# A scatter's integer places made by GpSimd instead of ScalarE, and the padding rows' scatters spread out

## The chip, the cores and the metric

The kernel runs on one core of one Trainium2 chip. The metric is the time of one execution on the device, in microseconds. A core has a matrix engine (PE, TensorE), three engines for elementwise work (DVE = VectorE, ACT = ScalarE, POOL = GpSimd) and a queue engine (SP = SyncE) that here issues most of the transfers between DRAM and on-chip memory. Each engine takes its own instructions in the order of the program; where one needs another's result it waits for a semaphore.

## What is computed

Two blocks follow each other. The first is a Fourier mixing of a batch of 8 sequences of 2496 positions with 256 features: a discrete Fourier transform along the features and one along the sequence, of which the real part is kept. The second is a mixture of experts over the resulting 19968 rows: each row goes to the one expert of 8 whose gate logit is largest, through two matrices with a ReLU between them, and is scaled by the gate's softmax weight.

```python
X = np.fft.fft(np.fft.fft(x, axis=1), axis=2).real      # x: (8, 2496, 256)
x = X.reshape(19968, 256)
logits = x @ w_gate                                     # (19968, 8)
e = argmax(logits, axis=1)
g = softmax(logits)[row, e]
out[row] = g * (maximum(x[row] @ w1[e], 0) @ w2[e])     # w1: (8, 256, 1024), w2: (8, 1024, 256)
```

## The kernel before

**Batches and rounds.** The 8 batches pass through the mixing one after the other (`first`, `regroup`, `second`), and the experts' work on batch b - 1 and older is woven with the mixing of batch b. `second` makes the mixed rows of a batch in two halves; each half has 10 tiles of 128 rows (`rows`, 258 wide: 256 values, the row's number, its gate weight). `route` (L416) finds each row's expert and, at L450 to L453, its place in the DRAM buffer `Xs`, where the rows lie sorted by expert.

**The scatters.** A tile's 128 rows go to their places by one indirect DMA from POOL, `put_row` (L235, its instruction has line L236): POOL reads 128 integers from a column of the tile `pi` and makes a transfer of them. `route` does not send at once; it appends the float place `pf`, the column of `pi` and the rows to the deque `waiting`, and `send` (L462) takes one entry off when the schedule says so. For the first batch DVE writes the integers in L453. For the other seven, ACT converts the float column to the integer column just before the scatter (L467). Seven batches of 20 tiles make 140 such conversions; the first batch has 20 scatters without one.

**When scatters are due.** The main loop (L941 to L971) steps through the experts' work and calls `send` after steps of the mixing; from batch 4 on (`LATE`, L184) a `room` count spaces them. For the batches before, an expert block that needs rows of a batch that is not yet complete makes the loop send everything that waits at once (L954 to L958). So scatters come in bursts, above all in the first three rounds.

**Reading the rows back.** `fetch_rows` (L524) has SP load a block of 512, 256 or 128 sorted rows. The first fetch of a batch waits until all its scatters have landed; later ones wait for a free buffer (`xb`, three of them). `turn` (L574) transposes the block on DVE (L580).

**Padding.** Blocks of the last round may run past an expert's rows. After the main loop, `pads` (L846) sends 8 scatters of padding rows, one for each expert, each yielding to the loop at L973: one scatter after each step of the experts' remaining work, so all eight within the first eight steps. Only the last round's blocks, fetched after it, need them.

**The last stage.** The blocks of the last round with 512 rows (`quartered`) take 21 steps each: 14 of the first layer (`seven`) and 7 of the second (`lower`). Each ends with four output scatters `out_dram<-y,ro` from POOL. POOL also makes, one block ahead, the combinations of the second layer's weights (`below`, `right`, L568 to L571) in these blocks.

**POOL's queue.** Every scatter, of rows, of padding and of output, is in one order on POOL. Each waits for the eighth scatter before it, as eight semaphores go round.

Of the kernel before, what the change touches and what calls it, by code (L numbers as in the profile page):

```python
# [12 lines left out]
F32 = mybir.dt.float32  # L13
# [202 lines left out]
def kernel(ctx: ExitStack, tc, x, w_gate, w1, w2, out):  # L216
    nc = tc.nc
    vec, act, pool = nc.vector, nc.scalar, nc.gpsimd
# [16 lines left out]
    def put_row(dst, idx, rows, last, group):  # L235
        return unordered(pool.indirect_dma_start(  # L236
            out=dst, out_offset=bass.IndirectOffsetOnAxis(ap=idx, axis=0),
            in_=rows, in_offset=None, bounds_check=last, oob_is_err=False), group)


    def sent(ins, b):
        tc.declare_no_dep(ins, group="taken", reason="no block before this batch's round has these rows")
        tc.add_to_no_dep_group(f"xs{b}", ins)
# [10 lines left out]
    sp = ctx.enter_context(tc.tile_pool(name="sp", bufs=2))  # L254
# [14 lines left out]
    con, k = {}, 0  # L269
# [192 lines left out]
    def send():  # L462

        if waiting:
            b, place, idx, rows = waiting.popleft()
            if b:
                act.copy(idx, place)  # L467
            sent(put_row(Xs, idx, rows, E * CAP - 1, "xs"), b)


# [375 lines left out]
    def pads(b):  # L846

        ti = cp.tile([128, E], I32, name="ti")
        vec.tensor_scalar(ti[:], base[:], con["lane"][:], None, op0=ALU.add)
        for e in range(E):  # L850
            sent(put_row(Xs, ti[:, e:e + 1], pad[:], ROWS - 1, "xs"), b)
            yield
# [82 lines left out]
    for k, _ in enumerate(second(0)):  # L935
        if k % 2 == 0:
            next(early, None)
        send()
    work = experts(todo)
    steps = {b: mixed(b) for b in range(1, B)}  # L940
    for b in range(1, B):  # L941

        done, due, room = 0, 0.0, 0.0
# [7 lines left out]
        while done < total:  # L951
            w, full = next(work)
            done += w
            if full and not w:  # L954

                while waiting:
                    send()
                whole.update(p[0] for p in tabs if p != "cnt")  # L958
            if not full:
                due += ticks * w / ((SHARE if b >= LATE else EARLY) * open_) if w else 1  # L960
            while due >= 1:
                next(side, None)
                due -= 1
                if b < LATE or not w:
                    send()
            room = min(room + (w if full else 0.75 * w), 2)
            if b >= LATE and room >= ROOM:
                send()
                room -= ROOM
        for _ in side:  # L970
            send()  # L971
    rest = pads(B - 1)
    for _ in work:  # L973
        next(rest, None)


_INS = ["x", "moe_w_gate", "moe_w1", "moe_w2"]
# [46 lines left out]
```

## Time and profile before

| | |
|---|---|
| median of 3 runs | 1304.29 us (1298.82 to 1309.32) |
| profiled execution | 1306.36 us, span of its instructions 1304.6 us |
| PE busy | 1227.3 us, 94% of the span |
| DVE, ACT, POOL busy | 700.7, 436.0, 361.8 us |
| scatters of rows, of padding, of output | 160, 8, 163 |
| mean granted clock of PE | 0.970 |

The profile is one execution. Its page lists each engine's busy time, a chain of waits followed back from the end, and groups of like instructions with their mean duration and the idle time of their engine before them. The timeline lists instructions with start and duration; in square brackets stands how long the engine was idle before, and what ended that. "issue" there means that the profile shows nothing that the engine waited for, "remote" that a semaphore came whose sender the profile could not match.

### The profile page before, as it was taken

Reading aid. Unit: us, or ns where it says so; the run is one execution under the profiler, and the core shown is the slowest. Engines: PE = TensorE matmul, PEld = TensorE weight load, DVE = VectorE, ACT = ScalarE, POOL = GpSimd, SP = SyncE. Lnnn points to the kernel's source line nnn. Section 1 sums busy time; section 2 is a strip of 40 time slices with the busy share of each in tenths; the row PEclk is TensorE's granted clock in tenths of the full one; section 3 lists DMA queues with packets and bytes.
Section 4 is the critical chain, followed back from the end, with each engine's and each line's share of the span. In section 5 each row is a group of like instructions: output and inputs, shape, how many; then the busy total and the mean of one; then the engine's idle time right before and its main releaser. Section 6 shows DMA issues by size and latency. Waiting matters only on the chain.

```text
span 1304.6 us, 21062 instructions
## 1 busy us (share of the span) xinstructions
PE 1227.3 (94%) x6905; PEld 1080.0 (83%) x6905; DVE 700.7 (54%) x1772; ACT 436.0 (33%) x1096; POOL 361.8 (28%) x355
## 2 busy tenths in 40 slices
PE   5668898999999999999999999999999999999996
PEld 3557797876788888888888888888889999999995
DVE  4455433433456555566546455675468774444662
ACT  1423222332334343434334343432233332222232
POOL 0245215125014311351114411351354221111112
PEclk8869898999999999999999999999999999999998
DMA  8859697657446445483335535453444238787786
GB/s 244 264 182 326 211 339 262 180 188 237 136 133 216 160 146 158 145 264 108 112 115 182 159 104 161 126 164 105 120 131 163 90 106 295 275 277 270 282 285 236
DMA packets 163210, 249.71 MB, mean 191 GB/s; under 512 B 118601, under 2 KB 130227, under 8 KB 143516
## 3 DMA queue, kind: packets, MB, share of 16 engines
q1 hardware_dynamic: 146327, 203.28, 49.0%
q0 software_dynamic: 15888, 42.14, 9.0%
q10 hardware_dynamic: 885, 2.94, 0.7%
q8 instruction: 56, 0.92, 0.3%
q14 instruction: 54, 0.44, 0.1%
HBM read 194.91 MB, written 54.83 MB: 191 GB/s over the span
## 4 chain that ended last, share of the span: by engine, by line
PE 86%; DVE 4%; DMA 4%; another core or an unknown queue 2%; issue 2%; ACT 1%; SPq 1%; POOL 0%; POOLq 0%; DVEq 0%; ACTq 0%
PE py L221 32%; PE ph L221 10%; PE c L221 10%; PE a L221 9%; PE p L221 6%; PE d L221 6%; PE b L221 5%; PE e L221 4%; PE s L221 3%; DMA w_sb<-in_moe_w_dram 2%; DMA xq<-in_x_dram 1%; DMA Td<-t 1%; SPq L532 1%; PE rk L221 0%
## 5 line engine op out<-in xcount | busy, mean ns | idle before, releaser
L221 PE MATMUL py<-w_sb,hT 128*128 128x256 f32 x2016 | 457.8, 381 | 8.3 <-DVE hT L794 8.3
L221 PEld LDWEIGHTS py<-w_sb,hT 128*128 128x128 f32 x2016 | 379.8, 191 | 59.1 <-DVE hT L794 8.7
L236 POOL DMA_INDIRECT out_dram<-y,ro x163 | 162.8, 999 | 735.8 <-ACT y L835 494.3
L236 POOL DMA_INDIRECT Xs<-rows,pi x160 | 163.5, 1022 | 199.0 <-ACT pi L467 81.6
L221 PE MATMUL ph<-xT,w_sb 128*128 128x128 f32 (+2 forms) x992 | 173.5, 330 | 9.0 <-DVE hT L794 5.3
L221 PEld LDWEIGHTS ph<-xT,w_sb 128*128 128x128 f32 x992 | 137.0, 194 | 34.3 <-issue 18.6
L835 ACT ACTIVATE y<-py,xb 128x256 f32<-128x256 f32 x129 | 61.1, 474 | 244.4 <-PE py L221 206.2
L221 PE MATMUL a<-xT,w_sb 128*128 128x256 f32 (+1 forms) x512 | 118.2, 358 | 2.1 <-ACT hT L629 1.3
L794 DVE TENSOR_SCALAR hT<-ph 128x512 f32<-128x512 f32 x43 | 29.7, 691 | 144.3 <-issue 73.6
L619 DVE TENSOR_TENSOR u<-p,b 128x512 f32<-128x512 f32 x57 | 39.2, 687 | 125.1 <-PE b L221 90.3
L221 PEld LDWEIGHTS a<-xT,w_sb 128*128 128x128 f32 x512 | 89.0, 190 | 14.7 <-ACT hT L629 2.5
L408 DVE COPY lg<-p 128x16 f32<-128x16 f32 x80 | 13.9, 174 | 142.4 <-ACT zs L405 131.8
L629 ACT ACTIVATE hT<-a 128x512 f32<-128x512 f32 x57 | 34.0, 597 | 157.7 <-PE a L221 116.7
L583 ACT ACTIVATE xT<-xT 128x256 f32<-128x256 f32 (+1 forms) x94 | 36.4, 387 | 135.3 <-DVE xT L580 88.6
L221 PE MATMUL s<-xq,w 104*112 104x256 f32 (+2 forms) x208 | 60.4, 413 | 13.1 <-DVE xq L297 12.6
L221 PEld LDWEIGHTS p<-table,t 120*128 120x128 f32 x352 | 55.3, 206 | 17.1 <-issue 6.3
L221 PE MATMUL c<-xT,ws 128*128 128x256 f32 (+1 forms) x256 | 60.5, 364 | 6.9 <-DVE hT L625 6.7
L221 PE MATMUL p<-table,t 120*128 120x120 f32 (+1 forms) x352 | 58.2, 292 | 8.3 <-ACT zz L379 3.4
L221 PE MATMUL p<-table,zz 128*128 128x145 f32 (+1 forms) x320 | 57.6, 305 | 7.8 <-issue 4.8
L580 DVE STREAM_TRANSPOSE xT<-xb 128x512 f32<-128x512 f32 (+1 forms) x94 | 58.1, 625 | 4.7 <-DMA xb<-Xs 4.7
L796 ACT ACTIVATE hT<-ph 128x512 f32<-128x512 f32 x55 | 32.8, 597 | 80.2 <-PE ph L221 59.1
L221 PE MATMUL b<-xs,ws 128*128 128x256 f32 (+1 forms) x256 | 58.7, 356 | 0.0
(145 smaller groups left out, 1739.8 us busy)
## 6 DMA issues: line engine op xcount, KB each, us to landing
w_sb<-in_moe_w_dram SPq DMA_DIRECT2D x132, 1024.0 KB
xq<-in_x_dram SPq DMA_DIRECT2D x24, 896.0 KB
xb<-Xs SPq DMA_DIRECT2D x112, 128.0 KB
Td<-t SPq DMA_DIRECT2D x18, 448.0 KB
t<-Td SPq DMA_DIRECT2D x8, 768.0 KB
t<-Td SPq DMA_DIRECT2D x8, 640.0 KB
xb<-Xs SPq DMA_DIRECT2D x52, 64.0 KB
xb<-Xs SPq DMA_DIRECT2D x100, 32.0 KB
```

The lines of the kernel that those rows point to most:

```text
L221: nc.tensor.matmul(o, lhsT=lhsT, rhs=rhs, start=start, stop=stop, **kw)
L236: return unordered(pool.indirect_dma_start(out=dst, out_offset=bass.IndirectOffsetOnAxis(ap=idx, axis=0), in_=rows, in_offset=None, bounds ...
L408: vec.tensor_copy(lg[:, k:k + 2], p3[:, NY:NY + 2 * E].rearrange("p (m e) -> p m e", m=2))
L532: taken(nc.sync.dma_start(out=flat[32 * q:32 * q + 32, 0:2 * size].rearrange("p (j e) -> p j e", e=64), in_=Xs[ds(row, size), 64 * q:64 * ...
L580: vec.transpose(free(xT[:], 256 * h, [32, n // 32], [BIG, 2], [1, 32]), free(xb, 512 * h, [64, n // 32], [1, 2], [2, 32]))
L583: act.activation(odd, odd, ACTF.Copy, scale=-1.0)
L619: vec.tensor_tensor(u2[:], p1[:], b[:], op=add)
L629: act.activation(h11, a[:], ACTF.Relu)
L794: vec.tensor_scalar(o, ph[:], 0.0, None, op0=ALU.max)
L796: act.activation(o, ph[:], ACTF.Relu)
L835: act.activation(y[:], py[:], ACTF.Copy, scale=meta[:, i, 1:2])
```

## The change

`send` gets a step more: ACT copies the float place into a small tile `due`, of which eight exist in turn, and POOL converts it into the integer column, directly before the scatter. The padding scatters are taken at every fourth step of the remaining work instead of at every one.

```diff
         if waiting:
             b, place, idx, rows = waiting.popleft()
             if b:
-                act.copy(idx, place)
+                due = sp.tile([128, 1], F32, tag="due", name="due", bufs=8)
+                act.copy(due[:], place)
+                pool.tensor_copy(idx, due[:])
             sent(put_row(Xs, idx, rows, E * CAP - 1, "xs"), b)
...
     rest = pads(B - 1)
-    for _ in work:
-        next(rest, None)
+    for k, _ in enumerate(work):
+        if k % 4 == 0:
+            next(rest, None)
```

In the built program ACT's copy now also waits for POOL's conversion of eight sends before, POOL's conversion waits for ACT's copy, and the scatter waits for POOL's own conversion. On PE, DVE and SP the order of the instructions is the same as before. On POOL four padding scatters stay in front of the second set of L568 to L571, a fifth comes behind it, and three come behind the four output scatters of the next block, in front of the third set.

## The prediction

> **What bounds the kernel.** I read the page first: engines and the chain of waits.
>
> ```profile
> span 1304.6 us, 21062 instructions
> PE 1227.3 (94%) x6905; PEld 1080.0 (83%) x6905; DVE 700.7 (54%) x1772; ACT 436.0 (33%) x1096; POOL 361.8 (28%) x355
> PE 86%; DVE 4%; DMA 4%; another core or an unknown queue 2%; issue 2%; ACT 1%; SPq 1%; POOL 0%; POOLq 0%; DVEq 0%; ACTq 0%
> ```
>
> PE is the bound, POOL has no share in the chain, and 2% (some 26 us) stands with an unknown sender. Both edits touch POOL and ACT, so the question is where these come into PE's way. The windows by stage (microseconds, then busy time of PE, PEld, DVE, ACT, POOL with instruction counts, granted PE clock, DMA share, GB/s) say where PE has holes:
>
> ```profile
> 52.00:90.00 38.00, 20.42 (x98) 16.77 (x96) 22.07 (x96) 9.88 (x32) 22.10 (x20) 0.64 0.62 203
> 90.00:145.00 55.00, 43.05 (x231) 36.57 (x232) 25.50 (x96) 16.19 (x60) 24.36 (x24) 0.91 0.85 280
> 145.00:236.00 91.00, 83.56 (x483) 74.56 (x484) 33.79 (x121) 26.52 (x84) 27.57 (x28) 0.94 0.83 281
> 236.00:960.00 724.00, 717.59 (x3519) 615.21 (x3518) 394.08 (x985) 265.86 (x666) 216.27 (x212) 1.00 0.50 156
> 960.00:1080.00 120.00, 119.26 (x858) 113.29 (x857) 96.38 (x174) 41.97 (x90) 36.10 (x32) 1.00 0.36 116
> ```
>
> From 236 us on PE is full: 100 of the 140 changed scatters (batches 3 to 7, 20 each) go out there, and PE idles 6.4 us of 724. The holes lie before 236 us. The timeline shows the largest:
>
> ```profile
> 125.20 2.75 PE L221 MATMUL py<-w_sb,hT 128*128 128x256 f32 x12
> 132.89 0.98 POOL L236 DMA_INDIRECT Xs<-rows,pi  x1 [0.30 <-issue]
> 135.50 0.69 DVE L794 TENSOR_SCALAR hT<-ph 128x512 f32<-128x512 f32 x1 [12.19 <-remote]
> 136.25 4.21 PE L221 MATMUL py<-w_sb,hT 128*128 128x256 f32 x9 [8.29 <-DVE hT L794]
> ```
>
> DVE's ReLU (L794) needs only matrix products whose last one started at 124.98, and yet its semaphore comes at 135.5. In that time POOL sends scatters one each 1.28 us; the last ends at 133.87. A second such pause stands at 208.25 to 213.59 (5.34 us of PE), again in a burst. After each pause the granted clock is 0.5 for a while. I call these **late semaphores in scatter bursts**; why they are late, the profile does not tell.
>
> **The change, part by part.**
>
> *ACT.* 140 casts of 189 ns become copies of one float column; the nearest copy (120x5 in L372) takes 173 ns. That is 140 x 16 ns = 2.2 us less on an engine that is 33% busy: nothing.
>
> *POOL.* Rows that bear on the price of one conversion:
>
> ```profile
> L236 POOL DMA_INDIRECT Xs<-rows,pi x160 | 163.5, 1022 | 199.0 <-ACT pi L467 81.6 <-DVE rows L410 53.7 <-issue 34.3
> L568 POOL TENSOR_TENSOR ws<-w_sb 128x512 f32<-128x512 f32 x5 | 6.5, 1291 | 0.2
> L1010 POOL MEMSET const-bfloat16-1.0<- 128x1 bf16 x1 | 0.1, 115 | 0.0
> ```
>
> A POOL instruction on one column is 0.115 us (the fill), on 512 columns 1.29 us. The conversion has one column, so I take 0.15 us. The scatter then waits for POOL's own semaphore; between L568 and L569, which have such a wait, lie 0.08 us. A scatter in a burst goes from 1.28 us to 1.28 + 0.15 + 0.08 = 1.51 us; the upper end is 1.28 + 1.29 + 0.08 = 2.65 us. 140 x 0.23 = 32 us of POOL work, beside 943 us in which POOL idles.
>
> Who waits for that? SP's first fetch of a batch waits for the last scatter. Batch 1's last starts at 141.34 and its fetch goes out at 159.27. Batch 2's fetch goes at 234.03 and DVE transposes the block at 258.74: 20 us of cover, against 20 x 0.23 = 4.6 us at most. Without that cover PE would wait those 4.6 us in each round.
>
> Queued behind ACT's copy, which now waits for the conversion eight sends before, are the ReLUs and PE's evictions. In the burst at 117 to 124 us ACT runs furthest ahead of POOL: the cast at 124.07 is 8.8 us before its scatter, seven scatters deep. At 1.51 us a scatter the eight tiles still suffice; at 2.0 ACT would stand 0.8 us. Elsewhere four are the most. Cost: nothing.
>
> In the full stretch (236 to 960 us), DVE can be held by a conversion for 0.15 us at a time. 100 x 0.15 = 15 us is 2% of that stretch; on the path I put 1 us (0 to 3). The row beside it is DVE's L778, which takes 1.32 us at 955.92 beside POOL's weight sums, and 0.69 us alone. The Trainium skill's page "SBUF — State Buffer", section "Who interferes with whom", speaks against the change here: a DVE instruction with two inputs in SBUF blocks against a GpSimd instruction that reads SBUF, which a conversion does and descriptor writing does not. By that rule every conversion may hold, or be held by, such a DVE instruction in full; if POOL's copy always met L306 (1.2 us here), a scatter would take 2.7 us.
>
> *The padding scatters.* They stand in a visible stall:
>
> ```profile
> 953.07 0.97 POOL L236 DMA_INDIRECT Xs<-pad,ti  x1 [0.30 <-issue]
> 954.05 1.29 POOL L568 TENSOR_TENSOR ws<-w_sb 128x512 f32<-128x512 f32 x1
> 955.31 0.69 DVE L625 TENSOR_TENSOR hT<-u,c 128x512 f32<-128x512 f32 x1 [2.14 <-remote]
> 955.92 1.32 DVE L778 TENSOR_TENSOR s<-s,hT 128x512 f32<-128x512 f32 x1
> 956.06 2.03 PE L221 MATMUL c<-xT,ws 128*128 128x256 f32 x4 [2.39 <-DVE hT L625]
> ```
>
> This is the same late semaphore, at the end of eight padding scatters in a row, with the clock at 0.5 until 959.6. In the windows of the two blocks, the one from 941.37 to 971.18 lasts 29.81 us with PE busy 26.77, and the next, 971.18 to 995.78, the same 21 steps without padding, 24.60. So the burst is worth up to 5.2 us. After the change four stay in that block in a row, then POOL's weight sums start at about 949 instead of 954; one more follows; three come behind the next block's four output scatters. Those three delay the third set of weight sums by 3 x 1.28 = 3.8 us, to 986.3; PE needs that set in the block after, at 1009.65, so 23 us cover it. SP's next two fetches wait for these scatters, but stand for a free buffer until 973.30 and 997.89, when they have long gone. I take 4 of the 5.2 us (0 to 5.2), since seven in a row now stand in the second block.
>
> *The late semaphores before 236 us.* PE idles 1.89 + 8.29 + 5.34 + 1.98 = 17.5 us in them (at 121.5, 128.0, 208.3, 230.7), and computes at half clock from 136.25 to 140.4 and from 213.6 to 218.9, which loses another 4.7: 22.2 us in all. Some 11 and 6 changed scatters stand in the two bursts. If a pause lasts as long as its burst, 17 x 0.23 = 4 us come on top (17 x 1.37 = 23 at the upper price). If the break before each scatter lets the queue run empty between two of them, up to 22 go. Nothing decides it; I take 0 and keep both ends. The burst of the first batch (54 to 82 us) has no conversion and stays.
>
> *Sum*, against the profiled 1306.36 us: 0 (ACT) + 0 (POOL behind cover) + 1 (DVE) - 4 (padding) + 0 (late semaphores) = 1303.4. That execution lies 2.1 us above the median of the three, so as a median **1301 us**. One per cent, 13 us, is about what a measurement of this kernel can tell from no change, since its three runs span 10.5.
>
> **Rivals.**
>
> *The pauses go.* A scatter that first waits for POOL's own conversion leaves the transfers time to drain. For it: both large pauses end within 2 us of their burst's last scatter or of its drain. Against it: the burst of batch 3 (291 to 317 us), as dense, has no pause. All gone: 1301 - 22 = 1279. Half gone: 1290. Chance 0.25.
>
> *The pauses grow* (the slower side). Semaphores come late in a burst, and the scatter now waits for one, POOL's own. At the upper price the two bursts last 23 us longer, and PE, DVE and ACT stand until they end: 1301 + 23 = 1324. It decides once a scatter in those bursts costs over 1 us more (17 scatters, 17 us, less the 4 of the padding). Against it: POOL's waits are already many there and it never misses its 1.28 us. Chance 0.16.
>
> *The spreading does not do what it says.* Four scatters in a row, then seven in the next block, may pause PE as eight did: 1305. Chance 0.2.
>
> **Chances and range.** My own case 0.39 and the third rival 0.2 lie within 1% of before: 0.59. Faster by more 0.25, slower by more 0.16. The range takes half to most of the first rival (down to 1281) and most of the second (up to 1319).
>
> **What would show it.** The conversions' group: mean near 150 ns. Scatters in a burst 1.5 us apart. POOL busy near 362 + 21 = 383 us. The block that starts at about 940 us near 26 us instead of 29.81. PE's holes near 128 and 208 us of the old size; if they are gone, the first rival holds, if each is over 10 us, the second. The prediction is wrong if the conversion takes over a microsecond, if ACT's copies wait for POOL, or if PE gets holes after 236 us.

## The result, and the profile after

| | before | after |
|---|---|---|
| median of five runs each | 1301.90 us (1298.82 to 1309.32) | 1285.14 us (1280.92 to 1291.36) |
| ratio to before, 95% interval | | 0.9862 [0.9832, 0.9892] |
| profiled execution, its span | 1306.36, 1304.6 us | 1280.92, 1279.1 us |

The changed kernel is 1.4% faster. The forecast said 1301 us and no measurable difference; its rival "the pauses go" had 1290 for half of them and 1279 for all. The page of the changed kernel, with the engines, the chain of waits and two groups:

```profile
span 1279.1 us, 21208 instructions
PE 1221.0 (95%) x6905; PEld 1077.0 (84%) x6905; DVE 700.4 (55%) x1772; ACT 436.3 (34%) x1096; POOL 398.3 (31%) x495
PE 87%; DMA 6%; DVE 3%; another core or an unknown queue 2%; issue 1%; ACT 1%; SPq 0%; POOL 0%; POOLq 0%; DVEq 0%; ACTq 0%
...
L221 PE MATMUL py<-w_sb,hT 128*128 128x256 f32 x2016 | 454.9, 380 | 1.3 <-DVE hT L796 1.3
...
L469 POOL CAST pi<-due 128x1 int32<-128x1 f32 x140 | 39.5, 282 | 69.1 <-ACT due L468 68.7
```

PE and DVE do the work of before, and POOL has its 140 conversions on top. The span is 25.5 us shorter, and 19.2 of these are idle time of PE: the second layer's products (`py`) stood 1.3 us for DVE's ReLU, where they stood 8.3 before. The other 6.3 us are busy time (1227.3 to 1221.0): in the kernel before the granted clock was 0.51 from 136.25 to 140.40 us and 0.50 from 213.60 to 218.90, right behind the two large pauses. The windows by stage of the changed kernel, in the columns of the prediction's table:

```profile
90.00:145.00 55.00, 48.90 (x272) 41.69 (x273) 26.93 (x102) 18.75 (x67) 29.26 (x44) 0.97 0.90 294
145.00:236.00 91.00, 88.75 (x531) 79.89 (x530) 36.52 (x128) 30.11 (x96) 35.34 (x50) 1.00 0.87 289
236.00:960.00 724.00, 722.71 (x3593) 623.32 (x3592) 406.52 (x1001) 267.50 (x664) 250.06 (x318) 1.00 0.49 155
```

From 90 to 236 us PE works 137.65 us where it worked 126.61, and from 145 us on its granted clock stays at 1.00 (0.94 before from 145 to 236). The order of PE's products is the same in both programs, so the time from one product to another can be compared directly. With the products that start at 91.37, 236.09, 941.37 and 995.78 us in the kernel before as marks:

| PE from mark to mark | before | after | gain |
|---|---|---|---|
| start to 91.37 | 91.37 | 90.01 | 1.4 |
| 91.37 to 236.09 (the two large pauses) | 144.7 | 130.7 | 14.0 |
| 236.09 to 941.37 (the full stretch) | 705.3 | 700.4 | 4.9 |
| 941.37 to 995.78 (the two blocks with the padding) | 54.4 | 50.7 | 3.7 |
| to the last product | 302.1 | 300.7 | 1.4 |

Of the 14.0 us, 9.9 are idle time of PE (18.0 before, 8.1 after) and 4.1 are busy time.

The timeline of the changed kernel shows the work that stood still in the first large pause before:

```profile
123.26 0.98 POOL L236 DMA_INDIRECT Xs<-rows,pi  x1 [0.28 <-issue]
124.23 0.20 POOL L469 CAST pi<-due 128x1 int32<-128x1 f32 x1
124.71 0.98 POOL L236 DMA_INDIRECT Xs<-rows,pi  x1 [0.28 <-POOL pi L469]
125.62 0.69 DVE L796 TENSOR_SCALAR hT<-ph 128x512 f32<-128x512 f32 x1 [2.43 <-remote]
...
126.37 1.99 PE L221 MATMUL ph<-xT,w_sb 128*128 128x256 f32 x8 [3.29 <-DVE hT L796]
...
131.54 0.69 DVE L796 TENSOR_SCALAR hT<-ph 128x512 f32<-128x512 f32 x1 [5.23 <-remote]
...
132.29 1.99 PE L221 MATMUL py<-w_sb,hT 128*128 128x256 f32 x8 [1.33 <-DVE hT L796]
```

The scatters now start every 1.46 us instead of 1.28, and DVE's ReLU starts while the burst still runs. Its semaphore is late, but by 2.4 and 3.2 us instead of 10.1 (from the end of the last product it needs to its start), and PE stands 3.29 and 1.33 us instead of 8.29. Late semaphores are not gone: an ACT ReLU between the two, at 128.62, comes 5.5 us after its product, while PE has other work. The second pause, 5.34 us, is 2.05 now. In all, PE's idle pieces of over 0.8 us between 100 and 1000 us sum to 8.9 us, from 21.5. The end of the padding in the changed kernel's timeline:

```profile
954.44 0.97 POOL L236 DMA_INDIRECT Xs<-pad,ti  x1 [0.30 <-issue]
...
955.42 1.29 POOL L570 TENSOR_TENSOR ws<-w_sb 128x512 f32<-128x512 f32 x1
...
958.32 1.13 PE L221 MATMUL c<-xT,ws 128*128 128x256 f32 x4 [1.18 <-DVE hT L627]
```

The last padding scatter ends 0.01 us before POOL's third set of weight sums, and PE waits 1.18 us for DVE here. The first of the two blocks takes 24.66 us instead of 29.82; the second, where four output scatters and three of padding now stand in a row (946.66 to 955.41), takes 26.04 instead of 24.59.

### The profile page after: what moved, and what is told of

It is laid out like the page before. It is cut to its first block, busy times and chain, and to the rows that moved or that the text cites. A ratio compares the mean times of both kernels' runs of the same rounds, so it can differ in the third digit from the quotient of the medians.

```text
span 1279.1 us, 21208 instructions
## 1 busy us (share of the span) xinstructions
PE 1221.0 (95%) x6905; PEld 1077.0 (84%) x6905; DVE 700.4 (55%) x1772; ACT 436.3 (34%) x1096; POOL 398.3 (31%) x495
## 4 chain that ended last, share of the span: by engine, by line
PE 87%; DMA 6%; DVE 3%; another core or an unknown queue 2%; issue 1%; ACT 1%; SPq 0%; POOL 0%; POOLq 0%; DVEq 0%; ACTq 0%
PE py L221 32%; PE ph L221 10%; PE c L221 10%; PE a L221 10%; PE p L221 6%; PE d L221 6%; PE b L221 5%; PE e L221 4%; PE s L221 3%; DMA xq<-in_x_dram 2%; DMA Td<-t 1%; DMA t<-Td 1%; DMA xb<-Xs 1%; PE rk L221 0%
## 5 line engine op out<-in xcount | busy, mean ns | idle before, releaser
L621 DVE TENSOR_TENSOR u<-p,b 128x512 f32<-128x512 f32 x57 | 39.1, 687 | 124.2 <-PE b L221 95.0
L469 POOL CAST pi<-due 128x1 int32<-128x1 f32 x140 | 39.5, 282 | 69.1 <-ACT due L468 68.7
```

What stands on the lines that cost most here:

```text
L469: pool.tensor_copy(idx, due[:])
L621: vec.tensor_tensor(u2[:], p1[:], b[:], op=add)
```

## The experiments

Kernels of one group ran on one chip, with the kernel before beside them; the three groups ran on three chips, here called 1, 2 and 3. "The stretch" is PE's time between the marks at 91.37 and 236.09 us, 144.7 us in the kernel before as first profiled. "Period" is the usual time from one scatter of rows to the next in the bursts behind the first batch.

### Chip 1: each part alone, a fill, and four conversions

The kernel before took 1304.27 us in the median of 23 runs here. First the padding alone, on the kernel before:

```diff
     rest = pads(B - 1)
-    for _ in work:
-        next(rest, None)
+    for k, _ in enumerate(work):
+        if k % 4 == 0:
+            next(rest, None)
```

> Only the padding scatters are spread; ScalarE still makes the integers. If late semaphores in scatter bursts cost the time and each burst costs for itself, the block with the padding scatters goes from 29.8 to some 26 us and the whole to 1302 - 4 = 1298 us (ratio 0.997); the large holes of PE before 236 us stay (17 us). If the padding was the main part of the gain, 1287 (0.989). If spreading them does nothing, 1302.

Measured: 1299.59 us, ratio 0.9973 [0.9953, 0.9993]. The two blocks take 50.0 us instead of 54.4, the stretch 144.4. Its timeline has both large pauses, at 8.21 and 4.64 us (8.29 and 5.34 before):

```profile
136.42 4.21 PE L221 MATMUL py<-w_sb,hT 128*128 128x256 f32 x9 [8.21 <-DVE hT L794]
...
213.10 3.78 PE L221 MATMUL ph<-xT,w_sb 128*128 128x256 f32 x8 [4.64 <-DVE hT L794]
```

So the padding is worth some 4 us, as forecast (the interval leaves 1 to 6), and the pauses reproduce. Then the conversion alone:

```diff
             if b:
-                act.copy(idx, place)
+                due = sp.tile([128, 1], F32, tag="due", name="due", bufs=8)
+                act.copy(due[:], place)
+                pool.tensor_copy(idx, due[:])
```

> Only the conversion moves to GpSimd; the padding scatters stay one per step. If the break between scatters shortens the late semaphores, PE's holes between 115 and 236 us fall from 17.5 to some 8 us as in the changed kernel, and the whole is 1285 + 4 = 1289 us (0.990); the padding block stays near 29.8 us. If the padding was the main part: 1298 (0.997).

Measured: 1286.63 us, ratio 0.9854 [0.9824, 0.9885], the stretch 134.8 us. The conversion carries nearly the whole gain. A pause of 6.15 us is left near 121.5 us in this execution; PE's idle pieces between 100 and 1000 us sum to 13.7 us, 3.9 of them at the padding. Next, a POOL instruction that nothing waits for, on the kernel before:

```diff
                 act.copy(idx, place)
+                gap = sp.tile([128, 1], F32, tag="gap", name="gap", bufs=8)
+                pool.memset(gap[:], 0.0)
```

> The kernel before, and GpSimd fills one scratch column (0.11 us) before each of the 140 scatters; the scatter does not wait for it, ScalarE still makes the integers, padding as before. If the spacing in time is what counts, a scatter in a burst comes each 1.39 us instead of 1.28 (1.46 in the changed kernel), and half or more of the gain is there: 1290 to 1296 us (0.991 to 0.996). If the scatter's wait for GpSimd's own semaphore is the brake, nothing: 1302 and PE's holes of 17 us as before.

Measured: 1305.29 us, ratio 0.9994 [0.9971, 1.0017], the stretch 145.4, a pause of 8.21 us again. POOL's timeline says why this tells less than it should:

```profile
124.05 0.12 POOL L469 MEMSET gap<- 128x1 f32 x1
124.36 0.97 POOL L236 DMA_INDIRECT Xs<-rows,pi  x1 [0.19 <-DMA Xs<-rows,pi]
```

The fill fits into the 0.30 us that lie between two scatters anyway, so the period stays 1.28 us. A POOL instruction between the scatters does nothing by itself; whether the time or the wait does it, this run can't tell. Last on this chip, more of the same:

```diff
-                pool.tensor_copy(idx, due[:])
+                for _ in range(4):
+                    pool.tensor_copy(idx, due[:])
```

> The changed kernel with the conversion made four times in a row, each waiting for the one before, so a scatter in a burst comes each 2.2 to 2.5 us. If the density of the scatters makes the late semaphores, PE's holes between 115 and 236 us fall below the 7.7 us of the changed kernel, to 3 or less, and the whole is 1275 to 1282 us (0.980 to 0.985), unless the later last scatter makes PE wait for rows. If the 1.46 us are enough already, 1285. If a longer burst costs more (the slower rival), over 1295.

Measured: 1288.78 us, ratio 0.9876 [0.9848, 0.9905], period 2.55 us. No compute semaphore is over 0.6 us late in the bursts of batches 1 and 2, and yet the stretch takes 135.4 us, for another reason. The timeline:

```profile
130.00 0.19 ACT L468 COPY due<-pf 128x1 f32<-128x1 f32 x1 [4.26 <-POOL pi L470]
...
134.75 0.19 ACT L468 COPY due<-pf 128x1 f32<-128x1 f32 x1 [2.35 <-POOL pi L470]
...
138.00 1.21 PE L221 MATMUL p<-table,t 120*128 120x120 f32 x4 [5.50 <-ACT t L372]
```

ACT's copies of the float wait for POOL to free one of the eight `due` tiles, and PE waits for an ACT copy queued behind them. A second stand of PE, 3.25 us before 220.18, has the same form: an ACT ReLU behind a copy that waited 3.41 us. That is the stall that the prediction priced for slow scatters and rightly took as nothing at 1.5 us.

### Chip 2: time without a wait, the first batch, and more tiles

The kernel before took 1296.07 us in the median of 11 runs. Four fills instead of one, still with no wait, and the padding as before:

```diff
                 act.copy(idx, place)
+                gap = sp.tile([128, 1], F32, tag="gap", name="gap", bufs=8)
+                for _ in range(4):
+                    pool.memset(gap[:], 0.0)
```

> The kernel before, with four POOL fills of one scratch column ahead of every scatter behind the first batch; none of them waits, and nothing waits for them. The fills took 126 ns each in the run with one fill, and one hid in the 0.30 us that lie between two scatters; four should not, and the scatters should come about every 1.28 + 4 x 0.126 - 0.30 = 1.48 us, close to the changed kernel's 1.46. Theory 'spacing in time' (the pauses ease because the scatters come less densely): 1286 to 1292, holes of PE near 128 and 208 us of half the old size or less. Theory 'own wait' (they ease because POOL waits for its own conversion, and so for the write of its result, ahead of each scatter): 1302 to 1308, holes near 128 and 208 us of 8 and 5 us as before. Padding is as in the kernel before, so the rest stays.

Measured: 1276.87 us, ratio 0.985 [0.9815, 0.9886]; the changed kernel beside it has 0.9869 (below). POOL's timeline, and the windows of the same run:

```profile
123.80 0.97 POOL L236 DMA_INDIRECT Xs<-rows,pi  x1 [0.71 <-issue]
124.76 0.60 POOL L470 MEMSET gap<- 128x1 f32 x4
```

```profile
90.00:145.00 55.00, 53.66 (x316) 47.30 (x315) 30.33 (x115) 21.53 (x75) 26.46 (x88) 0.97 0.94 317
145.00:236.00 91.00, 89.22 (x508) 79.44 (x508) 36.62 (x131) 29.17 (x90) 43.79 (x123) 0.98 0.82 272
```

The period is 2.27 us, not the 1.48 that I had worked out. PE works 142.88 us of the 146; the stretch takes 126.2 us, where the changed kernel on this chip takes 131.7 (below). What it wins there it loses at the padding, which is as before: the two blocks take 55.4 us, in the changed kernel 49.8. The scatter still waits for ACT's cast, as in the kernel before, and for nothing of POOL's. So **time between the scatters is enough; the wait for POOL's own conversion is not needed**. Since the period is longer than the changed kernel's, the run does not show that the wait adds nothing at 1.46 us.

Next, the conversion for the first batch too, on the changed kernel:

```diff
-        vec.tensor_tensor(pf[:] if b else pi[:], pf[:], con["far"][:, h], op=ALU.add)
+        vec.tensor_tensor(pf[:], pf[:], con["far"][:, h], op=ALU.add)
...
-            if b:
-                due = sp.tile([128, 1], F32, tag="due", name="due", bufs=8)
-                act.copy(due[:], place)
-                pool.tensor_copy(idx, due[:])
+            due = sp.tile([128, 1], F32, tag="due", name="due", bufs=8)
+            act.copy(due[:], place)
+            pool.tensor_copy(idx, due[:])
```

> The changed kernel, with the conversion for the first batch too: its places are written as floats by DVE, copied by ACT and turned into integers by POOL like the others. The first batch's scatters run from about 54 to 82 us, and PE stands there some 16 us in all, in the changed kernel and in the one before. Theory 'the late semaphores are the same there': the scatters' period in that burst grows from 1.28 to about 1.46 us and some 5 to 8 us of PE's standing go: 1277 to 1281. Theory 'PE stands there for its inputs (the transforms of the first batch come from a chain of loads and stores)': 1284 to 1287, holes as in the changed kernel.

Measured: 1280.62 us, ratio 0.9882 [0.9846, 0.9917], no better than the changed kernel. The first burst's period is 1.46 us and no compute semaphore in it is late by more than 0.6 us any more, but PE's idle time there is not shorter:

```profile
73.08 1.34 PE L221 MATMUL p<-table,zz 128*128 128x145 f32 x4 [7.41 <-ACT zz L379]
...
90.97 0.71 DVE L581 STREAM_TRANSPOSE xT<-xb 128x512 f32<-128x512 f32 x1 [7.18 <-DMA xb<-Xs]
...
91.74 1.65 PE L221 MATMUL ph<-xT,w_sb 128*128 128x256 f32 x3 [9.04 <-DVE ro L754]
```

Two waits have come in place of the late semaphores. The 7.41 us are the stall of the eight tiles again: ACT's copies of the float waited 8.2 us for POOL in this run, and an eviction stood behind them. The 9.04 us are the wait for rows: the first block can only be fetched when the last scatter has landed, and PE waits for that block. POOL scatters without a break up to there, so a burst that is stretched ends later (its last scatter starts at 84.54 us, in the unchanged repeat below at 80.71), and the block's products start at 91.74 instead of 90.02. The cover that this change has in later batches (20 us between a batch's last scatter and the use of its rows) is missing in the first.

The changed kernel once more, with no edit:

> The changed kernel once more, unchanged, beside the others on the same chip: 1285, with some 9 us of PE's holes between 100 and 1000 us, if its first profile was typical; the places of the small holes may move, the size of the two large ones of before (8 and 5 us) should not come back.

Measured: 1278.79 us, ratio 0.9869 [0.9835, 0.9904], the stretch 131.7 us, PE's idle pieces between 100 and 1000 us 5.7 us. The gain repeats, and neither large pause comes back. Then four conversions with 24 tiles:

```diff
-                due = sp.tile([128, 1], F32, tag="due", name="due", bufs=8)
+                due = sp.tile([128, 1], F32, tag="due", name="due", bufs=24)
...
-                pool.tensor_copy(idx, due[:])
+                for _ in range(4):
+                    pool.tensor_copy(idx, due[:])
```

> The run with four conversions per scatter, with 24 instead of 8 buffers for the float that ScalarE writes. There the scatters came every 2.55 us, no semaphore in the bursts was late, and PE stood 5.5 us near 132 us for an ACT copy, while ACT's own copies of the float waited 1.8 to 4.3 us each for POOL to free one of the eight buffers. Theory 'buffers': with 24 ACT waits for none of them, this hole goes, and the time falls by 3 to 6 us, to 1283 to 1286, at or below the changed kernel's. Theory 'it is a late semaphore under another name': the hole near 132 us stays, 1289.

Measured: 1282.67 us, ratio 0.9907 [0.987, 0.9944]. ACT's copies of the float no longer stand, PE's 5.5 us near 132 us are gone, and the stretch takes 129.9 us instead of 135.4: the buffers were the cause of that hole. That the time fell is not shown, since the two kernels ran on different chips and their ratios to the kernel before, 0.9907 and 0.9876, do not differ beyond their intervals. The whole is still 4 us slower than the changed kernel on the same chip. Some of that lies in the full stretch, which takes 703.7 us in this trace instead of 700.4.

### Chip 3: where the kernel before has nothing to gain

Here the kernel before took 1276.95 us in the median of 32 runs (1273.01 to 1281.37), 27 us less than on chip 1. Twelve fills ahead of every fifth scatter, none elsewhere:

```diff
                 act.copy(idx, place)
+                gap = sp.tile([128, 1], F32, tag="gap", name="gap", bufs=8)
+                for _ in range(0 if len(waiting) % 5 else 12):
+                    pool.memset(gap[:], 0.0)
```

> The kernel before, with twelve unwaited POOL fills ahead of every fifth scatter and none ahead of the others: four in five scatters still come 1.28 us after the one ahead, and each fifth about 1.28 + 11 x 0.33 = 4.9 us after it. The holes of the kernel before begin some 9 and 11 us after a run of twelve scatters at 1.28 us has begun. Theory 'it builds up' (scatters at 1.28 us go faster than something behind them works off, and semaphores come late when a run has been long enough, about eight): runs of five never reach it; the holes near 128 and 208 us are under 2 us and the time is 1282 to 1290 beside 1302 of the kernel before, in ratio 0.985 to 0.991. Theory 'each gap counts' (a semaphore gets through only in a gap between two scatters that is wider than 0.30 us): PE stands within each run of five, some 3 us per run, holes near 128 and 208 us of 3 to 5 us each, ratio 0.993 to 1.0.

Measured: 1274.85 us, ratio 0.9994 [0.9981, 1.0007]; each fifth scatter came 3.52 us after the one ahead, not 4.9. The theories can't be told apart by it, since there is no gain to share out. Read again, the trace of the kernel before does not bear out what I had put into the expectation either: its second pause begins after five scatters at 1.28 us, not twelve. Two fills per scatter (`range(2)`):

> The kernel before, with two unwaited fills per scatter: by the run with four (2.27 us, 0.33 for each fill behind the first, which costs nothing) the scatters come every 1.28 + 0.33 = 1.61 us, near the 1.46 of the run with the conversion alone. Theory 'spacing in time is all there is': as that run, ratio 0.984 to 0.989, holes of 13 us or less in all between 100 and 1000 us. Theory 'the wait for the conversion adds to it': at a like period the fills bring only part, ratio 0.990 to 0.996, and holes of 5 us or more near 128 us.

Measured: 1272.55 us, ratio 0.997 [0.9955, 0.9984]; the period was 1.95 us instead of the 1.61 expected. The same holds. Four fills, with the padding at every fourth step:

> Four unwaited fills per scatter on the kernel before, and the padding rows' scatters one per four steps. If the two parts add, this is the run with four fills (0.985 of the kernel before) less the 3 to 5 us of the padding: ratio 0.981 to 0.983, 1278 to 1281 where the kernel before takes 1303, with no hole near 940 us and under 4 us of holes between 100 and 1000 us; that is below the changed kernel by 3 to 6 us. If the padding's gain is hidden by something else once the rest is smooth: 0.985.

Measured: 1270.99 us, ratio 0.9958 [0.9944, 0.9972], the lowest time on this chip, 0.4% below the kernel before. The two blocks with the padding take 49.3 us, where the three other runs here, with a padding scatter at every step, take 50.8: here the padding is worth 1.5 us. The changed kernel did not run on this chip, so it is not shown that this version beats it. Last, the scattered rows cut to half, on the kernel before:

```diff
-    Xs = nc.dram_tensor("Xs", (ROWS, W), F32, kind="Internal").ap()
+    Xs = nc.dram_tensor("Xs", (ROWS, W - H), F32, kind="Internal").ap()
...
-            sent(put_row(Xs, idx, rows, E * CAP - 1, "xs"), b)
+            sent(put_row(Xs, idx, rows[:, H:], E * CAP - 1, "xs"), b)
...
-                in_=Xs[ds(row, size), 64 * q:64 * q + 64].rearrange("(j k) e -> k j e", k=32)), b)
+                in_=Xs[ds(row, size), 64 * (q % 2):64 * (q % 2) + 64].rearrange("(j k) e -> k j e", k=32)), b)
```

> The kernel before, with each scattered row cut to its second half and the two meta columns (130 of 258 columns); the blocks' loads read those 128 columns twice, so they move as many bytes as before and the transformed rows' first half is left out of the result. POOL's scatters stay as many, with 128 rows each. Theory 'bytes' (the late semaphores come from the scatters' transfers piling up on the DMA engines): with half the bytes the holes near 128 and 208 us shrink to under 3 us each, 1285 to 1294 where the kernel before takes 1303. Theory 'POOL's issue' (they come from the descriptors that POOL writes, whatever these move): scatters at 1.28 us, holes of 8 and 5 us, 1300 to 1305.

Measured: 1271.59 us, ratio 0.9967 [0.9955, 0.9979]; period 1.28 us, the stretch 124.4, no large pause. On a chip where the kernel before keeps its pauses this would speak for the bytes; here it says nothing of them.

That the late semaphores are missing on chip 3 can be read where the programs are the same: the first batch's scatters (54 to 82 us) come every 1.28 us, with no fill or conversion, in every kernel but that with the first batch converted. The timeline of the changed kernel on chip 2 there, ACT's evictions of PE's results (L379):

```profile
67.78 0.36 ACT L379 COPY zz<-p 128x240 f32<-128x240 f32 x1 [3.38 <-remote]
...
71.34 0.36 ACT L379 COPY zz<-p 128x240 f32<-128x240 f32 x1 [3.21 <-remote]
```

And that of the kernel with breaks on chip 3, the same instructions in the same burst:

```profile
61.87 0.98 POOL L236 DMA_INDIRECT Xs<-rows,pi  x1 [0.31 <-DVE p_nb L492]
...
62.54 0.36 ACT L379 COPY zz<-p 128x240 f32<-128x240 f32 x1 [0.87 <-PE p L221]
...
63.39 0.36 ACT L379 COPY zz<-p 128x240 f32<-128x240 f32 x1 [0.49 <-PE p L221]
```

On chip 3 these evictions start 0.04 us after the end of their product, in the middle of tight scatters; on chip 2 the two start 2.5 and 5.3 us after it, for a sender that the trace can't name. Between 50 and 100 us the four traces of chip 3 hold no instruction of DVE or ACT that starts over 0.6 us late (counted from the end of the last product of the tile that it reads, or from when its engine was free, whichever is later); the seven traces of chips 1 and 2 with this stretch unchanged hold five to nine each, those of the first pair seven each. The load of the DMA engines does not tell the two apart: from 54 to 84 us their busy share is 0.63 in the changed kernel of the first pair and 0.63 in the kernel with breaks on chip 3, and the packets of the scatters take 115 and 116 ns in the mean. No trace of the kernel before was taken in these three groups; that its two large pauses are missing on chip 3 is inferred from this and from its time.

## What was right and wrong in the prediction, by its steps

The measured 1285.14 us lies inside the stated range of 1281 to 1319, but my own sum, 1301, missed it by 16 us. The range holds it only because it was drawn to take in part of the first rival; my case, no difference that can be measured, did not come, and what came is that rival, in part, at a chance of 0.25. So the range was right without its reason.

**The late semaphores before 236 us: 0.** This is the step that failed. The stretch with them became 14.0 us shorter, of 22 that I had put up for it as one end. The reason that I gave for the gain, that a break before each scatter lets something drain, was on the page as a rival at 0.25; I set it to nothing because nothing on the page decided it. One sign was there: both late semaphores of the large pauses came when POOL had sent nothing for 1.6 and 1.5 us, and the conversion changes the scatters' spacing, whatever else it does. The mechanism of the rival was half right. Time between the scatters brings the gain (four fills, no wait: 0.985); the wait that I named is not needed. That it is the transfers that drain in this time, as the rival said, no run shows. Against the rival I had put the burst of batch 3, as dense and without a pause. That one burst goes well was no evidence that spacing does not help where it goes badly; and one semaphore is late there too, by 2.2 us (ACT's L835 at 303.9), while PE has other work.

**The full stretch: +1.** The sign was wrong: 705.3 us became 700.4. Single late semaphores stood there too: by the count above nine in the kernel before, 14.8 us in all, and two after, 1.4 us. On chip 3 the stretch takes 700.4 us in all four kernels.

**The conversion: 0.15 us, the period 1.51.** The conversion takes 0.20 us in the median and 0.282 in the mean, since 19 of 140 take over 0.5 us. The period is 1.46 = 0.98 + 0.20 + 0.28: the 0.30 us that lie between two scatters anyway shrink a little, so 0.18 us are added, not 0.23. POOL is busy 398.3 us instead of the 383 expected. No time between two marks grew, so POOL's longer work cost nothing, as forecast.

All 19 long conversions lie beside a DVE TENSOR_TENSOR with both inputs in SBUF (16 beside L565, 3 beside L306 and L296) and end 0.02 to 0.05 us after it. The timeline of the changed kernel has one:

```profile
395.48 0.69 DVE L565 TENSOR_TENSOR ws<-w_sb,ws 128x512 f32<-128x512 f32 x1
395.51 0.70 POOL L469 CAST pi<-due 128x1 int32<-128x1 f32 x1 [0.64 <-ACT due L468]
```

A conversion that starts 0.1 us or more ahead of such a sum is not long (0.18 to 0.23 us), and none is beside DVE's sums with an input in PSUM (L621, L624, L627, also 0.69 us). It is POOL that waits; DVE's sum has its usual 0.69 us. The Trainium skill's page "SBUF — State Buffer", section "Who interferes with whom", states this rule: a DVE instruction with two SBUF inputs blocks against a GpSimd instruction that reads SBUF. The trace agrees with it, with the 19 of 0.51 to 1.00 us. Its price here was small, since so few of the 140 meet such a sum and the engine that waits has slack.

**ACT: 0.** Right: 140 copies, 188 ns each, after 140 casts of 189. The eight tiles suffice at 1.46 us (no copy waited for one in the profiled pair, 1.5 us in all in the repeat); at 2.55 they do not, which cost PE 5.5 us in one place and 3.25 in another.

**The padding: -4.** Right in size: -3.7 in the profiled pair, 0.9973 alone on chip 1. Of what I had set against the gain, the second block's seven in a row cost 1.45 us of the 5.2 won in the first. The rival that the spreading would do nothing fell, and so did "the pauses grow": a burst that got longer paused less.

In sum, the profiled pair gained 25.4 us: 14.0 + 4.9 + 1.4 + 1.4 in stretches with late semaphores or around them, and 3.7 for the padding; by the medians the gain is 17, since the profiled execution before was one of the slower and that after the fastest of its five. My rival had 22 for all of the pauses before 236 us; the changed kernel got 14 of them, and 1285 lies between its 1279 and 1290.

**What stays open.** What holds the semaphores up, whether it builds up over a run of scatters or acts in each gap, and whether the bytes or POOL's issue matter: the runs for it met a chip on which next to nothing is late. Whether chip 3 differs as a chip, or something else in that session did, can't be told from one session each. What the change is worth there was not measured; the 0.4% of the fills with the padding is the nearest number.

## What to carry to other kernels

Where an engine stands for "remote" while another engine sends indirect transfers back to back, look at the spacing before the dependencies: 0.18 us more per scatter made a stretch of 145 us shorter by 14, although it lengthened the bursts there. Such spacing is free only where the last transfer of a burst has cover; where the next stage waits for it, as in the first batch, it brought nothing in the one run that tried it. Measure the kernel before on the same chip, and take a trace of it there: an edit that takes away a stall is worth nothing where the stall does not occur.

## What the runs showed of the hardware that I had not expected

- A semaphore from PE to DVE or ACT can come up to 10.1 us after the product that sends it while POOL issues scatters of 128 rows every 1.28 us. Between 100 and 236 us the lateness of the instructions of DVE and ACT that are over 0.6 us late, by the count above, sums to 28 to 29 us at a period of 1.28, to 10 to 17 at 1.46 and to under 1 at 2.27 and 2.55, on chips 1 and 2 and in the first pair; on chip 3 there is none at any period.
- The same kernel before took 1304, 1296 and 1277 us on three chips. The spread, 2%, is larger than the change's gain.
- One unwaited POOL fill of 0.126 us between two scatters costs nothing (the period stays 1.28 us); two add 0.67 us to the period and four 0.99.
